# One width of column tile for all products of a long convolution's main loop

## The chip, the cores and the metric

The kernel runs on one core of one Trainium2 chip. The metric is the device time of one execution in microseconds (us); lower is better.

## What is computed

Two parts follow each other. The first is a long convolution along the sequence, with a filter that a small network makes from positional features; the second lets a small expert network act on the 128 highest-scoring tokens of each batch.

```python
B, S, D = 4, 12608, 128                      # batch, sequence, channels; filter features 64
h_filt = (np.maximum(pos_emb @ w1, 0) @ w2) * np.exp(-0.01 * pos)[:, None]
u = x * v
y = irfft(rfft(u, n=2 * S, axis=1) * rfft(h_filt, n=2 * S, axis=0), n=2 * S, axis=1)[:, :S]
out = x * y                                  # [4, 12608, 128]

for b in range(B):                           # expert part, on x = out
    scores = x[b] @ w_gate
    top = np.argpartition(-scores, 128)[:128]
    xe = x[b, top]
    out[b, top] = xe + sigmoid(scores[top])[:, None] * (np.maximum(xe @ moe_w1, 0) @ moe_w2)
```

All of it is in float32.

## The kernel before, in words

The transforms are done as products with tables of sines and cosines. The length is factored as 101 x 250, so a transform has a stage over 101 points and one over 250 points, and real tables (sums of cosine and sine) keep it real. The 128 channels are taken in 32 groups of four, and with four batches that makes 128 iterations of the main loop, numbered t.

At the start the filter is made (`h_hid`, lines 254 to 334) and transformed (`h_spec`, lines 336 to 400); its spectra go to DRAM.

The main loop (lines 963 to 1024) is a pipeline written out by hand. In the iteration t TensorE gets, in this order:

- `f_i(t - 3)` (line 453), the inverse product of the group of three iterations before. For each of four channels and two halves (8 pairs) the helper `mm2` (line 237) multiplies a slice `sd[:, e, s]` of 101 columns, as the weights, with the table `ci_sb[:, e]` of 126 columns, as the moving operand. It does so in two parts: 51 columns to the PSUM partitions from 0 (line 240), and 50 columns to the partitions from 64 (line 241).
- `dft(t)` (line 243), the second stage: for each of two tables w, two halves of the 404 moving columns and two parities e, one product with 64 weight columns, to the partitions from 0 or from 64 (line 248).
- a small product of the background work, if one is due (`tots`, line 587, by way of `mm2`): while `spare` is set (lines 970 to 978), its result goes to the last 64 columns of two PSUM banks.
- `f_s1(t + 1)` (line 402), the first stage of the next group: for four channels and four blocks of 32 (the last has 29) weight columns one product of 202 moving columns, to the partitions from 0, 32, 64 and 96 (line 408).

In what follows these are called I (inverse), D (second stage) and S (first stage). A float32 product appears in the profile as two loads of weights and two matmul instructions. A product whose weights take at most 64 or 32 columns occupies only a column tile of that width of the TensorE array, and products in different column tiles run side by side.

The other engines work beside this. ScalarE copies from PSUM: D's second table (line 251), S's results in two halves (line 410), I's result into the large buffer `ay` (line 466). VectorE combines and multiplies with the filter's spectrum (lines 414, 417, 422, 423, 428, 429). GpSimd multiplies x and v (line 231) and prepares the inverse's input (lines 435 and 436). SyncE issues loads, some iterations ahead.

After each batch (32 inverse products) a phase between batches follows (class `P1`, lines 471 to 568): it takes the last transform stage from `ay` with the table `gx_sb` (lines 510 and 515, 64-wide column tiles), multiplies with x, writes the output and computes the scores. The rows of `ay` and of `gx_sb` stand in the partition layout that the inverse product leaves, which `_split` (line 66) gives to the table.

The search for the 128 highest scores of a batch (`TopKS`, `select`, `place`, lines 596 to 828) is spread as background work over the following batch's iterations by `Background` (line 572): each of its steps is a short piece on ScalarE, VectorE or GpSimd, and most rounds need one small product on TensorE between D and S. The last batch's search and the experts run at the end.

Of the kernel before, what the change touches and what calls it, by code (L numbers as in the profile page):

```python
# [18 lines left out]
NQ = 64  # L19
N1, N2, N3 = 101, 250, 125  # L20
N = N1 * N2
NJ = N2 // 2 + 1
# [14 lines left out]
LAG = 3  # L37
NU, NV, NX, NH = 4, 2, 4, 3
PR = 52
JH, KH = (N3 + 1) // 2, (N1 + 1) // 2  # L40
PJ = (N3 + 1) // 2
NC, CO = 4, 2
NE = 3
# [17 lines left out]
def _cas(m, n):  # L61
    t = 2.0 * np.pi * (m % n) / n
    return np.cos(t) + np.sin(t)


def _split(a, h):
    s = np.zeros((128,) + a.shape[1:])
    s[:h] = a[:h]
    s[NQ:NQ + len(a) - h] = a[h:]
    return s  # L70


def _grid():
    return (N3 * np.arange(N1)[:, None] + N1 * np.arange(N3)[None, :]) % (N1 * N3)


def _steps():
    j = np.arange(N3)
    first = -(-(N1 * N3 - N1 * j) // N3)
    blk = [slice(32 * k, min(32 * k + 32, N3)) for k in range(NB)]  # L80
    return first, [(c, int(first[c].min()), int(first[c].max())) for c in blk]


def _tables():
    kap = np.arange(N1) - N1 // 2
    idx = _grid()
    r1, r3 = idx[:, 0] % N1, idx[0] % N3
    rho, chi = (-1.0) ** np.arange(N1), (-1.0) ** (np.arange(N3) + r3)
    c1 = np.zeros((128, 1 + NB, N1))
    c1[:N1, 0] = _cas(r1[:, None] * kap[None, :], N1)  # L90
    alt = rho[:, None] * c1[:N1, 0]
    for k, (c, lo, hi) in enumerate(_steps()[1]):
        c1[:hi, 1 + k], c1[hi:N1, 1 + k] = alt[:hi], -alt[hi:]
        c1[N1:N1 + hi - lo, 1 + k] = -2 * alt[lo:hi]
    g = _cas(kap[:, None] * N2 * np.arange(GW)[None, :], N1)
    gx = _split(np.concatenate([g, -g], axis=1), KH)
    r = np.arange(NK)
    cf = np.zeros((N3, 2, 2, NQ))
    for e in range(2):
        ang = 2.0 * np.pi * ((r3[:, None] * (2 * r + e)[None, :]) % N2) / N2  # L100
        cf[:, 0, e, :NK] = np.cos(ang)
        cf[:, 1, e, :NK] = np.sin(ang)
    j = np.arange(NJ)
    ci = np.zeros((128, 2, NJ))
    for e in range(2):
        k = 2 * r + e
        wk = np.where((k == 0) | (k == N3), 0.5, 1.0)[:, None] / (2 * N)
        ang = 2.0 * np.pi * ((k[:, None] * j[None, :]) % N2) / N2
        ci[e * NQ:e * NQ + NK, 0] = np.cos(ang) * wk
        ci[e * NQ:e * NQ + NK, 1] = np.sin(ang) * wk  # L110
    fold = np.zeros((128, 2, NQ))
    fold[:JH] = cf[:JH, 0]
    fold[NQ:NQ + JH] = cf[:JH, 1]
    cf[:, :, 1] *= chi[:, None, None]
    win = np.exp(np.float32(-0.01) * np.arange(N1 * N3, dtype=np.float32))
    sg = np.where(idx % N2 < N3, 1.0, -1.0).astype(np.float32)
    wm = np.zeros((N1, 3, N3), np.float32)
    wm[:, 0] = np.where(idx < S, win[idx], 0.0)
    wm[:, 1] = sg
    wm[:, 2] = wm[:, 0] * sg  # L120
    p = np.arange(128)
    tk = np.zeros((128, 2 * 128 + 2 + 36 + NJ + 40), np.float32)
    tk[:, :128] = p[:, None] < p[None, :]
    tk[:, 128:256] = p[None, :]
    tk[:, 256] = NJ * np.where(p < NQ, p, np.maximum(p - NQ + PR, 0))
    tk[:, 257] = p + 1
    steps = np.array([[i << sh for i in range(4)] for sh in range(14, -1, -2)])
    steps = np.concatenate([steps, steps[:1] - 32768])
    tk[:, 258:294] = steps.reshape(1, -1)
    tk[:, 294 + NJ:] = np.concatenate([-steps[:8], 0.5 - steps[8:], 0.5 - steps[:1]]).reshape(1, -1)  # L130
    tk[:, 294:294 + NJ] = np.where(_valid(), -NEG, NEG)
    f = np.float32
    cf = np.concatenate([cf.reshape(N3, 4, NQ), np.zeros((128 - N3, 4, NQ))])
    return (fold.astype(f), c1.astype(f), gx.astype(f), cf.astype(f), ci.astype(f), wm, tk, np.zeros((NQ - PR, NX * 8 * D), f))
# [11 lines left out]
def _valid():  # L146
    ok = _index() < S
    ok[NQ:, 0] = ok[NQ:, NJ - 1] = False
    return ok
# [3 lines left out]
def hyena_moe(ctx, tc, xg, x2, pos, bw, ww, wg, mw1, mw2, fo, c1, gx, cf, ci, wm, tk, zr, out):  # L153
    nc = tc.nc
# [17 lines left out]
    def buf(name, k, shape):  # L172
        o, n, w = OFF[name]
        return view(arena, o + k % n * w, shape)
# [7 lines left out]
    def ps1(k, shape, name):  # L182
        return view((*bank1, *bank2[::2])[k], 0, shape)

    def ps2(k, shape, name):
        return view(bank2[k], 0, shape)
# [5 lines left out]
    cf_sb = cp.tile([128, 4, NQ], F32, name="cf_sb")  # L192
    ci_sb = cp.tile([128, 2, NJ], F32, name="ci_sb")
# [40 lines left out]
        if t < B * NG:  # L234
            nc.sync.dma_start(buf("ht", t, [128, 2 * HC]), hd[:, t % NG])

    def mm2(o, lhsT, rhs, h=NQ, **kw):
        kw = kw or dict(start=True, stop=True)
        m = lhsT.shape[1]
        nc.tensor.matmul(o[:h], lhsT=lhsT[:, :h], rhs=rhs, **kw)  # L240
        nc.tensor.matmul(o[NQ:NQ + m - h], lhsT=lhsT[:, h:], rhs=rhs, **kw)  # L241

    def dft(t, te, pq):
        for w in (1, 0):
            for h in range(2):
                c = slice(h * 2 * N1, (h + 1) * 2 * N1)
                for e in range(2):
                    nc.tensor.matmul(pq[w][e * NQ:(e + 1) * NQ, c], lhsT=cf_sb[:, 2 * w + e], rhs=te[:, e, c],  # L248
                                     start=True, stop=True)
        qs = buf("qs", t, [128, HC])  # L250
        nc.scalar.copy(out=qs, in_=pq[1])  # L251
        return qs
# [166 lines left out]
    def f_m(t, uv):  # L419
        ht = buf("ht", t, [128, 2, HC])  # L420
        mt = buf("mt", t, [128, 2, HC])
        nc.vector.tensor_tensor(out=mt, in0=uv, in1=ht[:, 0].unsqueeze(1).to_broadcast([128, 2, HC]), op=ALU.mult)  # L422
        nc.vector.tensor_tensor(out=uv, in0=uv, in1=ht[:, 1].unsqueeze(1).to_broadcast([128, 2, HC]), op=ALU.mult)  # L423
        return mt
# [28 lines left out]
    def f_i(t, sd):  # L453
        if t == B * NG - 1:
            for h in range(2):
                o3 = ps1(h, [128, 2, 256], f"o3_{t}_{h}")
                for s in range(2):
                    for e in range(2):
                        mm2(o3[:, s, e * NJ:(e + 1) * NJ], sd[:, e, 2 * h + s], ci_sb[:, e], KH)
                nc.scalar.copy(out=ay[:, t % NG, :, 2 * h:2 * h + 2], in_=o3[:, :, :2 * NJ].rearrange("p s x -> p x s"))  # L460
            return
        o3 = ps2(1 if t == B * NG - 2 else 2, [128, 4, 256], f"o3_{t}")
        for s in range(4):
            for e in range(2):
                mm2(o3[:, s, e * NJ:(e + 1) * NJ], sd[:, e, s], ci_sb[:, e], KH)
        nc.scalar.copy(out=ay[:, t % NG], in_=o3[:, :, :2 * NJ].rearrange("p s x -> p x s"))  # L466

    hbs = [(ja, min(HB, NJ - ja)) for ja in range(0, NJ, HB)]
# [101 lines left out]
    spare = [None]  # L570
# [16 lines left out]
    def tots(rhs, lhs, n, nm, k):  # L587
        parts = []
        for i, a in enumerate(range(0, n, NS) if spare[0] else (0,)):
            z = min(a + NS, n) if spare[0] else n  # L590
            ps = spare[0][i] if spare[0] else ps1(k, [128, 512], nm)
            mm2(ps[:, :z - a], lhs, rhs[:, a:z])
            parts.append((slice(a, z), ps[:, :z - a]))
        return parts
# [364 lines left out]
    te, uv, ys, sd, ph = {}, {}, {}, {}, {}  # L959
# [3 lines left out]
    for t in range(NT + LAG):  # L963
        g = t % NG
        i = t - LAG
        if 0 <= i:
            f_i(i, sd.pop(i))
        if t < NT:
            pq = ps2(1 - t % 2, [128, 2, 512], f"pq_{t}")
            spare[0] = [a[:, 512 - NS:] for a in bank1]  # L970
            uv[t] = pq[:, :, :HC]
            bg.now = t
            qs = dft(t, te.pop(t), (uv[t][:, 0], uv[t][:, 1]))
            bg.hook("p", 1)
            bg.hook("n", 1)
# [8 lines left out]
            o = t - 1 in uv  # L984
            if o:
                m = f_m(t - 1, uv[t - 1])
# [92 lines left out]
```

## Time and profile before

| | |
|---|---|
| median of 3 runs | 958.93 us (958.32 to 960.0) |
| the profiled execution's own time | 956.99 us |
| its span, first to last instruction | 955.2 us |
| TensorE clock granted, mean over the span | 0.989 |
| TensorE busy | 922.2 us, 15782 matmul instructions |
| VectorE, ScalarE, GpSimd busy | 824.8, 625.2, 633.1 us |
| moved by DMA | 194.44 MB |

In lines of the profile, PE is TensorE's matmuls and PEld its loads of weights, which overlap the matmuls; DVE is VectorE, ACT ScalarE, POOL GpSimd, SP SyncE. L408 is line 408 of the kernel. A group's line shows the result and the operands by the program's names, partitions x elements and type, the number of instructions after the x, then busy time in us, the mean length of one in ns, and the engine's idle time ahead of them with what ended it. In the timeline, a row holds a start, a length and how many instructions were merged; the bracket at its end is idle time before it and what ended it. The end of a matmul's record is modelled, and matmuls are pipelined, so starts are more to be trusted than ends.

### The profile page before, as it was taken

How to read it: one execution, taken by the hardware profiler on the slowest of the kernel's cores; microseconds unless marked ns; L12 is line 12 of the kernel's file. 1: busy time of each engine (PE TensorE's matmuls, PEld its weight loads, DVE VectorE, ACT ScalarE, POOL GpSimd, SP SyncE). 2: the span in 40 equal slices, each digit the busy share in tenths (PEclk: the TensorE clock that was granted, in tenths of full speed). 3: DMA queues.
4: the chain of work that ended last, by engine and by line, in shares of the span. 5: the costliest groups of instructions: out<-in, count | busy, mean ns of one | idle time of the engine just before them, and what ended most of it. 6: DMA issues, size and time to landing. Idle time of an engine off the chain costs nothing.

```text
span 955.2 us, 38707 instructions
## 1 busy us (share of the span) xinstructions
PE 922.2 (97%) x15782; PEld 763.7 (80%) x15782; DVE 824.8 (86%) x1585; ACT 625.2 (65%) x2085; POOL 633.1 (66%) x597
## 2 busy tenths in 40 slices
PE   7999999999999999999999999999999999999965
PEld 4788767777789987877799777777998878779954
DVE  5999988888889888889898888898998888987983
ACT  4755545555548987865578878755698878556930
POOL 2898556666669666667698466677893666767710
PEclk8999999999999999999999999999999999999997
DMA  7044587656777866567767666668687666765820
GB/s 217 21 175 177 207 279 187 231 197 195 234 221 237 277 213 213 196 197 230 236 223 271 221 197 199 198 202 266 199 272 248 197 199 191 226 180 156 270 80 7
DMA packets 81911, 194.44 MB, mean 204 GB/s; under 512 B 10697, under 2 KB 47662, under 8 KB 81710
## 3 DMA queue, kind: packets, MB, share of 16 engines
q1 hardware_dynamic: 81478, 191.45, 61.7%
q8 instruction: 124, 2.03, 0.9%
q0 software_dynamic: 256, 0.52, 0.2%
q14 instruction: 53, 0.43, 0.1%
HBM read 151.59 MB, written 40.34 MB: 201 GB/s over the span
## 4 chain that ended last, share of the span: by engine, by line
PE 87%; DMA 5%; DVE 4%; ACT 2%; issue 1%; SPq 0%; POOL 0%; POOLq 0%; DVEq 0%; ACTq 0%
PE c L240 24%; PE a L408 20%; PE c L248 18%; PE a L515 6%; PE c L384 3%; PE c L515 3%; PE a L364 3%; PE c L364 3%; PE a L510 2%; DMA arena<-in_x_dram 2%; DMA out_dram<-arena 2%; PE c L241 1%; DVE ms L636 1%; PE c L510 1%; DMA arena<-in_pos_dram 1%
## 5 line engine op out<-in xcount | busy, mean ns | idle before, releaser
L435 POOL TENSOR_TENSOR arena<-arena 128x404 f32<-128x404 f32 x127 | 123.1, 969 | 228.1 <-DVE arena L429 193.4
L240 PEld LDWEIGHTS c<-ci_sb,arena 128*51 128x51 f32 x2032 | 213.8, 125 | 44.8 <-issue 20.0
L240 PE MATMUL c<-ci_sb,arena 128*51 128x126 f32 x2032 | 245.3, 273 | 4.3 <-ACT big L466 2.3
L241 PE MATMUL c<-ci_sb,arena 128*50 128x126 f32 x2032 | 245.2, 273 | 0.0
L241 PEld LDWEIGHTS c<-ci_sb,arena 128*50 128x50 f32 x2032 | 213.6, 124 | 0.0
L408 PE MATMUL a<-c_sb,arena 128*32 128x202 f32 (+1 forms) x4096 | 202.7, 336 | 0.0
L248 PE MATMUL c<-arena,cf_sb 128*64 128x202 f32 x2048 | 198.2, 334 | 1.1 <-ACT arena L410 1.1
L466 ACT COPY big<-c 128x1008 f32<-128x1008 f32 x127 | 125.7, 990 | 96.7 <-PE c L241 93.5
L410 ACT COPY arena<-a 128x404 f32<-128x404 f32 x256 | 127.5, 498 | 74.6 <-PE a L408 74.5
L408 PEld LDWEIGHTS a<-c_sb,arena 128*32 128x32 f32 (+1 forms) x4096 | 120.4, 108 | 60.4 <-issue 17.8
L231 POOL TENSOR_TENSOR arena<-arena 128x500 f32<-128x500 f32 x128 | 161.1, 1259 | 9.2 <-DMA arena<-in_xg_dram 9.2
L248 PEld LDWEIGHTS c<-arena,cf_sb 128*64 128x64 f32 x2048 | 141.2, 136 | 25.2 <-ACT arena L410 2.8
L547 ACT ACTIVATE arena<-arena 128x128 f32<-128x128 f32 x496 | 147.2, 298 | 18.3 <-DVE arena L545 15.5
L498 POOL TENSOR_TENSOR arena<-big 128x512 f32<-128x512 f32 x112 | 139.9, 1275 | 10.2 <-ACT big L460 2.8
L422 DVE TENSOR_TENSOR arena<-c,arena 128x808 f32<-128x808 f32 x127 | 126.8, 998 | 3.9
L417 DVE TENSOR_TENSOR c<-c,arena 128x404 f32<-128x404 f32 x128 | 75.0, 586 | 61.4 <-ACT arena L251 61.4
L423 DVE TENSOR_TENSOR c<-c,arena 128x808 f32<-128x808 f32 x127 | 126.7, 998 | 0.0
L436 POOL TENSOR_TENSOR arena<-arena 128x404 f32<-128x404 f32 x127 | 123.5, 972 | 0.0
L515 PE MATMUL a<-big,gx_sb 128*64 128x128 f32 x1536 | 97.0, 273 | 0.7 <-ACT big L460 0.7
L547 ACT ACTIVATION_READ_ACCUMULATOR arena<-arena 128x1 f32 x496 | 92.7, 187 | 0.0
L251 ACT COPY arena<-c 128x404 f32<-128x404 f32 x128 | 63.5, 496 | 39.0 <-PE c L248 34.4
L515 PEld LDWEIGHTS a<-big,gx_sb 128*64 128x64 f32 x1536 | 86.2, 137 | 2.1 <-ACT arena L410 1.0
(198 smaller groups left out, 1407.0 us busy)
## 6 DMA issues: line engine op xcount, KB each, us to landing
arena<-in_xg_dram SPq DMA_DIRECT2D x256, 250.0 KB
arena<-hd SPq DMA_DIRECT2D x128, 404.0 KB
arena<-in_x_dram SPq DMA_DIRECT2D x120, 208.0 KB
out_dram<-arena SPq DMA_DIRECT2D x120, 208.0 KB
hd<-arena SPq DMA_DIRECT2D x32, 404.0 KB
arena<-in_pos_dram SPq DMA_DIRECT2D x15, 202.0 KB
arena<-in_x_dram SPq DMA_DIRECT2D x8, 156.0 KB
out_dram<-arena SPq DMA_DIRECT2D x8, 156.0 KB
```

Source lines behind the costliest of these rows:

```text
L231: nc.gpsimd.tensor_tensor(out=x, in0=x, in1=v, op=ALU.mult)
L240: nc.tensor.matmul(o[:h], lhsT=lhsT[:, :h], rhs=rhs, **kw)
L241: nc.tensor.matmul(o[NQ:NQ + m - h], lhsT=lhsT[:, h:], rhs=rhs, **kw)
L248: nc.tensor.matmul(pq[w][e * NQ:(e + 1) * NQ, c], lhsT=cf_sb[:, 2 * w + e], rhs=te[:, e, c], start=True, stop=True)
L408: nc.tensor.matmul(tps[s // 2][c, s % 2], lhsT=u[:, s, c], rhs=c1_sb[:, 0:k + 2:k + 1], start=True, stop=True)
L410: nc.scalar.copy(out=te[:, :, 2 * h:2 * h + 2].rearrange("p e s i -> p s e i"), in_=tps[h])
L422: nc.vector.tensor_tensor(out=mt, in0=uv, in1=ht[:, 0].unsqueeze(1).to_broadcast([128, 2, HC]), op=ALU.mult)
L423: nc.vector.tensor_tensor(out=uv, in0=uv, in1=ht[:, 1].unsqueeze(1).to_broadcast([128, 2, HC]), op=ALU.mult)
L466: nc.scalar.copy(out=ay[:, t % NG], in_=o3[:, :, :2 * NJ].rearrange("p s x -> p x s"))
L498: nc.gpsimd.tensor_tensor(out=cm[e][:, :n].rearrange("p j (g s) -> p j g s", s=4), in0=av[0], in1=av[1], op=op)
L515: nc.tensor.matmul(ps[t * NQ:(t + 1) * NQ, k], lhsT=gx_sb[:, o:o + NQ], rhs=ay[:, :, e * NJ + j], start=e == 0, stop=e == 1)
L547: nc.scalar.activation(out=wx[:, k], in_=wx[:, k], func=AF.Copy, accum_out=self.sc[:, ja + k:ja + k + 1])
```

## The change

All products of I, D and S use column tiles that are 32 wide.

- I: a slice of 101 weight columns is multiplied in four parts of 26, 25, 25 and 25 columns, to the partitions from 0, 32, 64 and 96, by the new helper `mm4`. `_split` gives the table `gx` the same layout of rows.
- D: for each table there are four products of 32 weight columns, each with all 404 moving columns of its parity, in place of two halves with two products of 64 weight columns each.
- The small products of the background work take four parts of 32 columns while `spare` is set (in the main loop), and two parts of 64 elsewhere, as before.

```diff
+KQ = [slice(int(c[0]), int(c[-1]) + 1) for c in np.array_split(np.arange(N1), 4)]
-def _split(a, h):
+def _split(a):
     s = np.zeros((128,) + a.shape[1:])
-    s[:h] = a[:h]
-    s[NQ:NQ + len(a) - h] = a[h:]
+    for k, c in enumerate(KQ):
+        s[32 * k:32 * k + c.stop - c.start] = a[c]
     return s
...
-    def mm2(o, lhsT, rhs, h=NQ, **kw):
+    def mm2(o, lhsT, rhs, **kw):
         kw = kw or dict(start=True, stop=True)
-        m = lhsT.shape[1]
-        nc.tensor.matmul(o[:h], lhsT=lhsT[:, :h], rhs=rhs, **kw)
-        nc.tensor.matmul(o[NQ:NQ + m - h], lhsT=lhsT[:, h:], rhs=rhs, **kw)
+        w = 32 if spare[0] else NQ
+        for a in range(0, 128, w):
+            nc.tensor.matmul(o[a:a + w], lhsT=lhsT[:, a:a + w], rhs=rhs, **kw)
+
+    def mm4(o, lhsT, rhs):
+        for k, c in enumerate(KQ):
+            nc.tensor.matmul(o[32 * k:32 * k + c.stop - c.start], lhsT=lhsT[:, c], rhs=rhs, start=True, stop=True)
 
     def dft(t, te, pq):
         for w in (1, 0):
-            for h in range(2):
-                c = slice(h * 2 * N1, (h + 1) * 2 * N1)
-                for e in range(2):
-                    nc.tensor.matmul(pq[w][e * NQ:(e + 1) * NQ, c], lhsT=cf_sb[:, 2 * w + e], rhs=te[:, e, c],
-                                     start=True, stop=True)
+            for a in range(0, 128, 32):
+                nc.tensor.matmul(pq[w][a:a + 32], lhsT=cf_sb[:, 2 * w + a // NQ, a % NQ:a % NQ + 32],
+                                 rhs=te[:, a // NQ], start=True, stop=True)
...
         for s in range(4):
             for e in range(2):
-                mm2(o3[:, s, e * NJ:(e + 1) * NJ], sd[:, e, s], ci_sb[:, e], KH)
+                mm4(o3[:, s, e * NJ:(e + 1) * NJ], sd[:, e, s], ci_sb[:, e])
```

The last group's inverse, which is done in two halves, changes in the same way.

More of the change, by code (lines that the diff above doesn't have):

```diff
@@ L39 @@
 PR = 52
-JH, KH = (N3 + 1) // 2, (N1 + 1) // 2
+JH = (N3 + 1) // 2
 PJ = (N3 + 1) // 2
@@ L95, in _tables @@
     g = _cas(kap[:, None] * N2 * np.arange(GW)[None, :], N1)
-    gx = _split(np.concatenate([g, -g], axis=1), KH)
+    gx = _split(np.concatenate([g, -g], axis=1))
     r = np.arange(NK)
@@ L458, in f_i @@
                     for e in range(2):
-                        mm2(o3[:, s, e * NJ:(e + 1) * NJ], sd[:, e, 2 * h + s], ci_sb[:, e], KH)
+                        mm4(o3[:, s, e * NJ:(e + 1) * NJ], sd[:, e, 2 * h + s], ci_sb[:, e])
                 nc.scalar.copy(out=ay[:, t % NG, :, 2 * h:2 * h + 2], in_=o3[:, :, :2 * NJ].rearrange("p s x -> p x s"))
```

## The prediction

> **What bounds the kernel now.** I read the page first, then one iteration of the main loop in the timeline, then groups of instructions by shape, the list of waits, and busy time by window.
>
> ```profile
> span 955.2 us, 38707 instructions
> PE 922.2 (97%) x15782; PEld 763.7 (80%) x15782; DVE 824.8 (86%) x1585; ACT 625.2 (65%) x2085; POOL 633.1 (66%) x597
> PE 87%; DMA 5%; DVE 4%; ACT 2%; issue 1%; SPq 0%; POOL 0%; POOLq 0%; DVEq 0%; ACTq 0%
> ```
>
> TensorE is busy 97% of the span and holds 87% of the chain that ended last. A busy TensorE isn't one that streams all the time, so I look inside an iteration (timeline, TensorE alone; columns are start and length in us):
>
> ```profile
> 200.77 1.58 PE L408 MATMUL a<-c_sb,arena 128*32 128x202 f32 x32
> 202.28 0.31 PE L240 MATMUL c<-ci_sb,arena 128*51 128x126 f32 x1
> ...
> 202.43 0.27 PE L240 MATMUL c<-ci_sb,arena 128*51 128x126 f32 x1
> ...
> 203.94 0.27 PE L240 MATMUL c<-ci_sb,arena 128*51 128x126 f32 x1
> ...
> 204.05 1.54 PE L248 MATMUL c<-arena,cf_sb 128*64 128x202 f32 x16
> 205.51 1.58 PE L408 MATMUL a<-c_sb,arena 128*32 128x202 f32 x32
> ```
>
> Start to start, the first stage S (L408, four column tiles of 32) takes 202.28 - 200.77 = 1.51 us, the inverse I (L240 and L241, two tiles of 64) 1.77, the second stage D (L248, two tiles of 64) 1.46: 4.74 us in all. Each float32 product is two matmul instructions, so S is 8 rounds of four tiles (32 instructions), D is 8 rounds of two (16), and I is 16 rounds of two.
>
> What would the streaming alone take? The mean lengths by shape tell:
>
> ```profile
> L240 PE MATMUL c<-ci_sb,arena 128*51 128x126 f32 x2032 | 245.3, 273 | 4.3 <-ACT big L466 2.3 <-POOL arena L435 1.6 <-POOL arena L436 0.5
> L408 PE MATMUL a<-c_sb,arena 128*32 128x202 f32 x3072 | 202.7, 337 | 0.0
> L241 PE MATMUL a<-st,onesb 128*64 128x3 bf16 x48 | 8.0, 166 | 0.0
> ```
>
> 76 more columns cost 337 - 273 = 64 ns, so a column costs 0.842 ns: a round of 202 columns streams in 0.170 us, one of 126 in 0.106. The rest of a record is latency that overlaps the next round. Inside I the rounds stand (203.94 - 202.43) / 14 = 0.108 us apart, so there the estimate holds. D and S should take 8 x 0.170 = 1.36 each and I 16 x 0.108 = 1.73, together 4.45. The measured 4.74 has 0.29 more: 0.10 at the end of D, 0.15 in S, 0.04 in I's first round (202.28 to 202.43 is 0.15, not 0.108).
>
> Two rows show that this loss belongs to the joint between tile widths. In the phase between batches, two 64-wide lines alternate:
>
> ```profile
> 300.56 1.04 PE L515 MATMUL a<-big,gx_sb 128*64 128x128 f32 x16
> 301.43 0.61 PE L510 MATMUL a<-arena,gx_sb 128*64 128x128 f32 x8
> 301.87 1.04 PE L515 MATMUL a<-big,gx_sb 128*64 128x128 f32 x16
> 302.74 0.61 PE L510 MATMUL a<-arena,gx_sb 128*64 128x128 f32 x8
> ```
>
> 8 rounds of 128 columns in 0.87 us and 4 in 0.44: 0.109 a round by 0.842 x 128 = 0.108, nothing lost at the joints. And in iterations with a background step, a tiny 64-wide product stands between D and S:
>
> ```profile
> 404.13 1.54 PE L248 MATMUL c<-arena,cf_sb 128*64 128x202 f32 x16
> 405.50 0.17 PE L240 MATMUL a<-st,onesb 128*64 128x3 bf16 x1
> ...
> 405.60 1.58 PE L408 MATMUL a<-c_sb,arena 128*32 128x202 f32 x32
> ...
> 408.88 0.34 PE L248 MATMUL c<-arena,cf_sb 128*64 128x202 f32 x2
> ```
>
> D lasts 405.50 - 404.13 = 1.37 when a 64-wide product follows it, against 1.46 when a 32-wide one does. So 0.1 us is lost where 64 goes over to 32, and as much where 32 goes over to 64. The waits of the weight loads count these joints:
>
> ```profile
> PEld c L240 <- issue: 20.2, 63, 0.3
> PEld a L408 <- issue: 17.8, 63, 0.3
> PEld c L240 <- POOL arena L231: 15.9, 49, 0.3
> PEld a L408 <- POOL arena L436: 10.0, 54, 0.3
> ```
>
> 117 times a load of S and 112 times a load of I came up to 0.3 us late, whatever releaser the view names.
>
> **The change, part by part.** *Joints.* With I, D and S all 32 wide, both joints of an iteration go. Worth: 117 x 0.10 (D to S) + 112 x (0.15 + 0.04) (S to I) = 11.7 + 21.3 = 33 us. The Trainium skill (TensorEngine Tiling, section Tiling Modes, Key Properties) says that a change of tiling mode drains TensorE; this trace agrees with its 0.10 and 0.19 us, and the sum uses these.
>
> *D.* Eight rounds of two tiles and 202 columns become four rounds of four tiles and 404 columns: 4 x 404 x 0.842 = 1.36 us, as now; 16 loads and 16 matmuls as now. Zero. The copy that waits for D (L251) starts after D's last matmul: the last round starts 0.17 us earlier than now and its record is 0.17 longer, so L251 stays where it is, counted from D's start.
>
> *I.* Sixteen rounds of two tiles become sixteen of four (26, 25, 25, 25 columns). Streamed columns are unchanged, but 32 + 32 instructions become 64 + 64. What must hold is 8 instructions per 0.108 us, 13.5 ns each, and no row of before shows that over a whole stage. From below the round is 0.106 (streaming). From above: S, with four tiles, issues 64 instructions in 1.36 us, 21 ns each, and at that rate a round takes 0.170. I take 0.108, because S shows that four tiles don't lengthen a round: 1.36 / 8 = 0.170 with four, 1.37 / 8 = 0.171 with two. And where instructions stand ready, they go out much faster. This is the window of 60 ns from 205.50:
>
> ```profile
> 205.51 0.15 PEld L408 LDWEIGHTS a<-c_sb,arena 128*32 128x32 f32 x7 [0.30 <-issue]
> 205.51 0.38 PE L408 MATMUL a<-c_sb,arena 128*32 128x202 f32 x4
> ```
>
> Eleven instructions in some 50 ns. So the 21 ns of S is its streaming and not a rate of issue. For the range I use up to 0.118 a round, a tenth more: 16 x 0.010 x 118 = 19 us.
>
> *The small products of the background step* (48 iterations by the row of 48 above, and a few longer ones) become 32 wide in four parts. Today they hide in the drain: that iteration is 408.88 - 404.13 = 4.75, as long as a plain one. With the drain gone they stand in the open: between 0 and the 0.10 from 405.50 to 405.60, in which the switch is still included. I take 0.04: 48 x 0.04 = 2 us. At 64 wide they would bring two switches, about 0.2.
>
> *The phase between batches* stays 64 wide, so where it hands over to I there is now a joint that wasn't: nearest row S to I, 0.15 + 0.04, three times, 0.6 us. The constants' rows in gx and the rows of the copied inverse move with the parts; no instruction is added for that.
>
> *What is late next.* An iteration shrinks to about 4.46 (4.50 with a background step). Busy time by window, for a plain iteration, one with a background step, and the ten that hold a selection:
>
> ```profile
> 204.05:208.80 4.75, 4.75 (x85) 3.70 (x83) 3.96 (x7) 2.49 (x4) 3.11 (x4) 1.00 0.61 201
> 404.13:408.88 4.75, 4.75 (x86) 3.80 (x84) 4.13 (x9) 4.02 (x14) 3.11 (x4) 1.00 0.58 188
> 418.39:466.32 47.93, 47.93 (x822) 38.05 (x820) 43.53 (x82) 25.02 (x41) 34.48 (x36) 1.00 0.72 226
> ```
>
> The columns are length, then PE, PEld, DVE, ACT, POOL, the clock, the share and rate of DMA. DVE needs 3.96 and 4.13 (ACT 4.02), so 0.3 stays free. The ten iterations become 47.9 - 2.7 = 45.2 against 43.5 of DVE, still free on the whole, but single ones are full. DVE may run late there without holding TensorE much: 1 us in all. DMA moves 201 GB/s in 61% of the time and would move 6% more. In a background iteration ACT's order is the tight place:
>
> ```profile
> 404.63 0.98 ACT L466 COPY big<-c 128x1008 f32<-128x1008 f32 x1
> 405.72 0.50 ACT L251 COPY arena<-c 128x404 f32<-128x404 f32 x1
> 406.25 0.59 DVE L417 TENSOR_TENSOR c<-c,arena 128x404 f32<-128x404 f32 x1 [0.32 <-ACT arena L251]
> 407.09 0.17 DVE L708 SCALAR_TENSOR_TENSOR st<-a,tk_sb 128x3 f32<-128x3 f32 x1 [0.26 <-ACT arena L410]
> ```
>
> L466 ends at 405.61 and L251 starts at 405.72. Up to 0.1 us of lateness of L251 would come out of DVE's idle 0.32 and 0.26, not out of TensorE's time.
>
> *Sum.* 33 - 2 - 0.6 - 1 = 29.4, taken as 30 because the ten longer background products (a few rounds each) lose a drain as well. The profiled execution took 956.99 us (span 955.2 and 1.8 around it), so it would take 927; the median of the runs is 958.9, 0.2% above it, so the forecast is **929 us**.
>
> **Rivals.** *A, slower: TensorE's issue becomes I's bound.* It decides from where an instruction takes more than (1.73 + 0.29) / 128 = 15.8 ns over the stage. For it: the fastest whole stages of before issue 64 instructions in about 1.4 to 1.5 us,
>
> ```profile
> 54.56 1.61 PE L364 MATMUL a<-c_sb,arena 101*63 101x101 f32 x32
> 56.09 0.92 PE L384 MATMUL c<-arena 63*64 63x202 f32 x16
> ```
>
> here 32 matmuls and as many loads in 1.53 us. Against it: this stage streams 16 x 101 x 0.842 = 1.36 anyway, and the burst above. Price at S's 21 ns: I takes 2.69, an iteration 0.67 more than now, 118 x 0.67 = 79: 1038 us. Chance 9%. The Trainium skill (TensorEngine Tiling, Instruction Overhead) puts about 60 cycles on each matmul, 25 ns by its clock of 2.4 GHz; for matmuls alone I would need 64 x 25 = 1.6 us and still fit, with the loads charged too 3.2 us, and the kernel would be near 1100. The seven loads and four matmuls in 60 ns speak against that reading.
>
> *B, no change: the joints stay.* If the late load at a joint came from a semaphore, as the POOL names in the waits suggest, nothing would go, and the background product would even cost: 957 to 960 us. Against it: I to D also waits for another engine's semaphore, and loses nothing (203.94 to 204.05 is a normal 0.11). Chance 6%.
>
> *C, a slower round.* Four parts lengthen I's round to 0.118 to 0.130, with half or all of the gain eaten: 948 to 970. Chance 11%, most of it below 957.
>
> **How the numbers follow.** Forecast 74%, A 9%, B 6%, C 11%. From below, 33 us, no cost for background products and rounds of 0.106 (118 x 0.03 = 3.5) give 37, 921.9 us, taken as 921. From above the forecast reaches C's 948. Range 921 to 948, which leaves out A, B and C's tail. About 0.2% is what a measurement here can tell from no change. Faster by more: 74 + 8 of C + 2 of B = 84%. Within: 5%. Slower: A and 2 of C, 11%.
>
> **What would show it.** Right: in the timeline of after, D, S and I of about 1.36, 1.37 and 1.73 us, an iteration of 4.46; no idle of 0.3 before the first loads of S and I; D as long before S as before a background product. Wrong: rounds of I over 0.118 (A or C), the 0.1 still there at the joints (B), or TensorE idle in front of D with DVE or ACT named as releaser.

## The result and the profile after

The changed kernel takes 929.03 us (median of 4 runs, 926.76 to 932.16); beside it the kernel before took 959.46 (4 runs, 958.32 to 962.25). The ratio is 0.968, interval 0.964 to 0.972. The profiled execution took 927.64 us, against 956.99 before: 29.35 less. Measured a second time, beside other variants, the changed kernel took 931.38 us (6 runs) against 958.82, ratio 0.972 (0.970 to 0.974).

The page of the changed kernel: the span, the busy times, the queue that carries instructions (packets, MB, share of 16 DMA engines), and the shares of the chain that ended last.

```profile
span 925.9 us, 47199 instructions
...
PE 892.9 (96%) x20028; PEld 813.4 (88%) x20028; DVE 824.1 (89%) x1585; ACT 624.1 (67%) x2085; POOL 634.6 (69%) x597
...
q8 instruction: 157, 2.57, 1.1%
...
PE 87%; DMA 5%; DVE 4%; issue 2%; ACT 2%; SPq 0%; POOL 0%; POOLq 0%; DVEq 0%; ACTq 0%
```

TensorE has 4246 more matmuls and is busy for 29 us less; the other engines do what they did. The chain is as much TensorE's as before. One row is worth remembering for later: 2 x 20028 instructions (matmuls and loads) in 157 packets are 255 to a packet, and 2.57 MB / 157 are 16.4 KB each. With the 314 further instructions of TensorE that the trace has (semaphores, drains) it is 257. So TensorE's instructions arrive in chunks of some 256.

One iteration in the timeline, TensorE alone (start, length, operation, number of instructions):

```profile
132.96 1.57 PE L253 MATMUL c<-arena,cf_sb 128*32 128x404 f32 x16
134.31 1.61 PE L413 MATMUL a<-c_sb,arena 128*32 128x202 f32 x32
135.68 1.97 PE L248 MATMUL c<-ci_sb,arena 128*26 128x126 f32 x64
137.41 1.59 PE L253 MATMUL c<-arena,cf_sb 128*32 128x404 f32 x16
```

Start to start, D takes 134.31 - 132.96 = 1.35, S 1.37, I 1.73: the streaming times, with nothing left at the joints. Sixteen rounds of I with four tiles last as long as sixteen with two did.

Busy time by window (length, then PE, PEld, DVE, ACT, POOL, the clock, DMA's share and rate) for a plain iteration, one with a background step, and the ten that hold a selection:

```profile
202.40:206.87 4.47, 4.47 (x120) 4.39 (x115) 3.96 (x7) 2.49 (x4) 3.12 (x4) 1.00 0.87 289
389.47:393.97 4.50, 4.50 (x124) 4.28 (x119) 4.14 (x9) 3.99 (x13) 3.12 (x4) 1.00 0.64 209
411.94:457.00 45.06, 45.06 (x1153) 43.59 (x1148) 42.89 (x78) 24.95 (x41) 34.14 (x36) 1.00 0.80 244
```

TensorE is busy all the time in each; VectorE has 45.06 - 42.89 = 2.2 us left over the ten iterations, and no stage of them waits for it.

The list of waits of the weight loads, whole run (total, times, longest):

```profile
PEld c L253 <- issue: 8.3, 44, 0.2
PEld a L413 <- issue: 5.7, 29, 0.3
...
PEld c L248 <- issue: 2.8, 9, 0.5
```

Before, loads of S came late 117 times and loads of I 112 times, by up to 0.3 us. Now it is 29 and 9. The 44 short waits ahead of D are new, but a load that comes 0.2 us later stops nothing here: the matmuls of the stretches above are busy without a gap. The 0.5 in the last row is new too; it falls into the iterations that zr_split, below, is about.

### The profile page after: what moved, and what is told of

Read it like the earlier page. It is cut to its first block, busy times and chain, and to the rows that moved or that the text cites. A ratio compares the mean times of both kernels' runs of the same rounds, so it can differ in the third digit from the quotient of the medians.

```text
span 925.9 us, 47199 instructions
## 1 busy us (share of the span) xinstructions
PE 892.9 (96%) x20028; PEld 813.4 (88%) x20028; DVE 824.1 (89%) x1585; ACT 624.1 (67%) x2085; POOL 634.6 (69%) x597
## 3 DMA queue, kind: packets, MB, share of 16 engines
q8 instruction: 157, 2.57, 1.1%
## 4 chain that ended last, share of the span: by engine, by line
PE 87%; DMA 5%; DVE 4%; issue 2%; ACT 2%; SPq 0%; POOL 0%; POOLq 0%; DVEq 0%; ACTq 0%
PE c L248 23%; PE a L413 20%; PE c L253 18%; PE a L520 7%; PE c L520 3%; PE c L389 3%; PE a L369 3%; PE c L369 3%; PE a L515 3%; DMA out_dram<-arena 2%; DVE ms L641 1%; PE c L515 1%; DMA arena<-in_wm_dram 1%; DMA arena<-in_x_dram 1%; PE c L244 1%
## 5 line engine op out<-in xcount | busy, mean ns | idle before, releaser
L248 PE MATMUL c<-ci_sb,arena 128*26 128x126 f32 x8128 | 269.2, 271 | 4.8 <-ACT big L471 2.1
L248 PEld LDWEIGHTS c<-ci_sb,arena 128*26 128x26 f32 x8128 | 250.2, 104 | 10.0 <-ACT big L471 3.3
L413 PE MATMUL a<-c_sb,arena 128*32 128x202 f32 (+1 forms) x4096 | 223.9, 334 | 0.0
L253 PE MATMUL c<-arena,cf_sb 128*32 128x404 f32 x2048 | 220.4, 502 | 2.2 <-ACT arena L415 1.3
L413 PEld LDWEIGHTS a<-c_sb,arena 128*32 128x32 f32 (+1 forms) x4096 | 186.5, 108 | 18.5 <-issue 5.7
L253 PEld LDWEIGHTS c<-arena,cf_sb 128*32 128x32 f32 x2048 | 119.0, 109 | 22.2 <-issue 8.3
L422 DVE TENSOR_TENSOR c<-c,arena 128x404 f32<-128x404 f32 x128 | 75.0, 586 | 37.8 <-ACT arena L256 37.5
L550 DVE TENSOR_TENSOR arena<-arena,c 128x512 f32<-128x512 f32 x124 | 83.9, 678 | 0.2 <-ACT arena L552 0.2
L419 DVE TENSOR_TENSOR c<-c,arena 128x404 f32<-128x404 f32 x128 | 74.3, 580 | 0.1
```

The source lines that it names most:

```text
L248: nc.tensor.matmul(o[32 * k:32 * k + c.stop - c.start], lhsT=lhsT[:, c], rhs=rhs, start=True, stop=True)
L253: nc.tensor.matmul(pq[w][a:a + 32], lhsT=cf_sb[:, 2 * w + a // NQ, a % NQ:a % NQ + 32], rhs=te[:, a // NQ], start=True, stop=True)
L413: nc.tensor.matmul(tps[s // 2][c, s % 2], lhsT=u[:, s, c], rhs=c1_sb[:, 0:k + 2:k + 1], start=True, stop=True)
```

## The experiments

The theory after the result: the 0.29 us of an iteration were lost at the joints between column tiles of 32 and of 64, and the change gains because no joint is left. Rivals: the four parts of I, or the long moving operand of D, are faster by themselves. A second question is how near rival A of the prediction is: what does TensorE's issue bear?

### One stage at a time: i_only and d_only

In i_only, D and the small products go back to tiles of 64; I and S are 32 wide.

```diff
-        w = 32 if spare[0] else NQ
+        w = NQ
...
-            for a in range(0, 128, 32):
-                nc.tensor.matmul(pq[w][a:a + 32], lhsT=cf_sb[:, 2 * w + a // NQ, a % NQ:a % NQ + 32],
-                                 rhs=te[:, a // NQ], start=True, stop=True)
+            for h in range(2):
+                c = slice(h * 2 * N1, (h + 1) * 2 * N1)
+                for e in range(2):
+                    nc.tensor.matmul(pq[w][e * NQ:(e + 1) * NQ, c], lhsT=cf_sb[:, 2 * w + e], rhs=te[:, e, c],
+                                     start=True, stop=True)
```

> Only the inverse I is cut into four 32-wide parts; D and the small background products stay 64 wide as before the change. Joint theory: the joint S to I goes (0.19 us), but I to D becomes a new one of the same kind (32 to 64, 0.15 to 0.19 us), and D to S stays, so an iteration stays at 4.70 to 4.76 us and the time at 955 to 961 us. Rival 'narrow tiles are faster by themselves': I is one of the two stages made narrow, so about half of the gain, 940 to 947 us. Rival 'the long moving operand of D': no gain without D, 957 to 961 us, so this run doesn't tell it from the joints. If four parts lengthened I's round, the time would lie over 961 us.

It took 961.16 us (10 runs), ratio 1.002 (1.0005 to 1.0035), far from the rival's 940 to 947 and 0.2 us above the range, where a longer round of I had been the sign; but I's round is 0.108 us in the changed kernel too. An iteration of it in the timeline:

```profile
205.01 1.59 PE L255 MATMUL c<-arena,cf_sb 128*64 128x202 f32 x16
206.53 1.58 PE L415 MATMUL a<-c_sb,arena 128*32 128x202 f32 x32
207.92 1.92 PE L248 MATMUL c<-ci_sb,arena 128*26 128x126 f32 x64
209.77 1.59 PE L255 MATMUL c<-arena,cf_sb 128*64 128x202 f32 x16
```

D 1.52, S 1.39, I 1.85: 4.76, the old total. S has lost its extra time to I, whose next neighbour, D, now is the one of another width. The joint has moved.

In d_only, I goes back to two parts of 51 and 50 columns, while D and the small products stay 32 wide.

```diff
-KQ = [slice(int(c[0]), int(c[-1]) + 1) for c in np.array_split(np.arange(N1), 4)]
+KQ = [slice(int(c[0]), int(c[-1]) + 1) for c in np.array_split(np.arange(N1), 2)]
...
-            nc.tensor.matmul(o[32 * k:32 * k + c.stop - c.start], lhsT=lhsT[:, c], rhs=rhs, start=True, stop=True)
+            nc.tensor.matmul(o[NQ * k:NQ * k + c.stop - c.start], lhsT=lhsT[:, c], rhs=rhs, start=True, stop=True)
```

> Only D (four products of 404 columns) and the small background products are 32 wide; I stays in two 64-wide parts. Joint theory: D to S has no joint any more, I to D gets one (64 to 32, 0.10 us and a longer first round), S to I keeps its own: an iteration of about 4.75 us, 956 to 963 us. Rival 'the long moving operand of D' or 'narrow D': the whole gain, 928 to 932 us, or the half of it, 940 to 947 us.

959.31 us (10 runs), ratio 1.0004 (0.9985 to 1.0022). The timeline:

```profile
203.64 1.56 PE L253 MATMUL c<-arena,cf_sb 128*32 128x404 f32 x16
205.02 1.56 PE L413 MATMUL a<-c_sb,arena 128*32 128x202 f32 x32
206.51 1.94 PE L248 MATMUL c<-ci_sb,arena 128*51 128x126 f32 x32
208.37 1.56 PE L253 MATMUL c<-arena,cf_sb 128*32 128x404 f32 x16
```

D, with its 404 columns and beside S of the same width, takes 1.38; S 1.49 and I 1.86 hold the two joints now. Neither part alone gains anything, so neither the four parts of I nor the long moving operand of D is faster by itself; only both together take the last joint away.

### A 64-wide speck in a 32-wide loop: tots64

Only the small products of the background step go back to 64.

```diff
-        w = 32 if spare[0] else NQ
+        w = NQ
```

> The changed kernel, but the small background products stay 64 wide, in two parts. Joint theory: the 48 iterations with a round of the search and 9 with a longer product get two joints each, 0.15 to 0.25 us in an iteration: 48 such iterations of 4.65 to 4.70 instead of 4.50 us, the time 937 to 943 us. If width did not matter at a joint: 928 to 930 us.

941.32 us (4 runs), ratio 0.9816 (0.9795 to 0.9836). A background iteration in the timeline:

```profile
394.74 1.55 PE L253 MATMUL c<-arena,cf_sb 128*32 128x404 f32 x16
396.22 0.20 PE L244 MATMUL a<-st,onesb 128*64 128x3 bf16 x2
396.34 1.58 PE L413 MATMUL a<-c_sb,arena 128*32 128x202 f32 x32
397.73 1.92 PE L248 MATMUL c<-ci_sb,arena 128*26 128x126 f32 x64
399.46 1.55 PE L253 MATMUL c<-arena,cf_sb 128*32 128x404 f32 x16
```

Two tiny products bring the iteration from 4.50 to 4.72, where 4.65 to 4.70 was expected. D lasts 1.48 instead of 1.35, and S starts 0.12 after them. 48 such steps at 0.22 are 10.6 us of the 12.3 between the two medians. It is the change of width that costs, not the work: the same product in four parts of 32 costs an iteration 0.03.

### More instructions: d_halves

D keeps its tiles of 32 but does its 404 columns in two halves: as many columns, twice the instructions in D, 256 in an iteration instead of 224.

```diff
-            for a in range(0, 128, 32):
-                nc.tensor.matmul(pq[w][a:a + 32], lhsT=cf_sb[:, 2 * w + a // NQ, a % NQ:a % NQ + 32],
-                                 rhs=te[:, a // NQ], start=True, stop=True)
+            for h in range(2):
+                c = slice(h * 2 * N1, (h + 1) * 2 * N1)
+                for a in range(0, 128, 32):
+                    nc.tensor.matmul(pq[w][a:a + 32, c], lhsT=cf_sb[:, 2 * w + a // NQ, a % NQ:a % NQ + 32],
+                                     rhs=te[:, a // NQ, c], start=True, stop=True)
```

> The changed kernel, but D multiplies two halves of 202 moving columns with four 32-wide weights each (twice the instructions, eight rounds of four tiles instead of four). Joint theory: streamed columns and widths are the same, so an iteration of 4.46 to 4.49 us and 928 to 932 us. Rival 'the long moving operand of D': most of the gain is lost, 945 to 959 us.

A miss: 962.3 us (10 runs), ratio 1.0034 (1.0015 to 1.0054). All the gain is gone, although the undisturbed iteration is 4.48, as expected. By the time alone this looks like the rival, the long moving operand; but by that rival every iteration would be longer, and d_only had the long operand without a gain. What is lost lies in stops: 41 of the iterations hold some, 33 us together. One in the timeline:

```profile
164.99 0.84 PE L415 MATMUL a<-c_sb,arena 128*32 128x202 f32 x10
168.33 1.06 PE L415 MATMUL a<-c_sb,arena 128*32 128x202 f32 x19 [2.50 <-issue]
```

In the middle of S, 2.50 us pass with nothing to wait for that the profile shows. The DMA view of 135 to 275 us has the two queues that matter, data and instructions:

```profile
q1 hardware_dynamic: 13130, 29.01, 70.5%
q8 instruction: 29, 0.48, 1.4%
```

At 4.48 us an iteration and 256 instructions in each, these 140 us need 140 / 4.48 = 31.3 chunks; 29 came. That alone proves nothing, for a TensorE that stands still needs fewer instructions, but it suggests a second theory: the chunks share the DMA engines with the data, and one that comes late stops TensorE (supply). Its rival: the doubled instructions of D stop TensorE in some way of their own, whatever DMA carries.

### Less data beside the instructions: after_noh and d_halves_noh

Take away the load of the filters' spectra (404 KB in every iteration) from the moment all of their buffers have been filled.

```diff
     def load_h(t):
-        if t < B * NG:
+        if t < NH:
```

> The changed kernel without 404 KB of the 904 KB that each iteration loads: after the first three groups the filter spectrum isn't loaded again, and later groups are multiplied with the spectra that lie in the three buffers, so the result isn't the convolution. It is the control for the next run. The transfers aren't on the path that sets the end: 925 to 929 us. If late instruction chunks (theory of supply) cost the changed kernel some 2 us, they go: 925 to 927.

> The changed kernel with D in halves of 202 columns (256 TensorE instructions in an iteration in place of 224), and again without the reloads of the filter spectrum after the first three groups (later groups use the spectra that lie there). Theory of supply: TensorE's instructions arrive in chunks of 16 KB (256 instructions) over the same DMA engines as the data, a chunk that waits behind data comes late, and TensorE stands still; with 45% less data the stops mostly go: 929 to 938 us. Theory of issue: TensorE itself can't take 256 instructions in 4.48 us: 955 to 964 us, as with the loads. Theory of a fetch with a limit of its own, whatever the data: 955 to 964 us too.

after_noh: 927.45 us (4 runs), ratio 0.9678 (0.9653 to 0.9702). d_halves_noh: 932.86 (4 runs), ratio 0.976 (0.972 to 0.980). The control, after_noh, has the changed kernel's ratio, 0.968: fewer loads gain nothing that the runs can tell. But d_halves_noh, with the same instructions as d_halves, got some 29 us back, and the stops shrank to about 5 us in 8 iterations. Busy time by window over the same 140 us, first d_halves, then d_halves_noh:

```profile
135.00:275.00 140.00, 134.27 (x3766) 129.68 (x3762) 115.90 (x178) 72.99 (x118) 90.49 (x87) 0.99 0.72 211
```

```profile
135.00:275.00 140.00, 138.92 (x3955) 136.82 (x3946) 122.27 (x186) 76.98 (x125) 96.92 (x93) 1.00 0.46 132
```

DMA's rate falls from 211 to 132 GB/s, and TensorE's idle time from 140 - 134.27 = 5.7 us to 1.1. Nothing on TensorE was changed between the two, so its stops come by way of the transfers. The theory of issue falls, and so does that of a fetch that can't bear 256 instructions in 4.48 us whatever the data.

### Twice the instructions in I: i_halves and i_halves_noh

I's 126 moving columns in two halves of 63: 256 instructions in I, 352 in an iteration, streamed columns unchanged. It puts rival A to the test at twice the rate of issue.

```diff
-        for k, c in enumerate(KQ):
-            nc.tensor.matmul(o[32 * k:32 * k + c.stop - c.start], lhsT=lhsT[:, c], rhs=rhs, start=True, stop=True)
+        n = NJ // 2
+        for j in range(0, NJ, n):
+            for k, c in enumerate(KQ):
+                nc.tensor.matmul(o[32 * k:32 * k + c.stop - c.start, j:j + n], lhsT=lhsT[:, c], rhs=rhs[:, j:j + n], start=True, stop=True)
```

> The changed kernel with I's moving operand in two halves of 63 columns: 256 instructions in I (8 in 0.053 us, 6.6 ns each), 352 in an iteration. Theory of supply: where TensorE had stopped, chunks of 256 followed each other every 4.2 to 4.3 us, so an iteration takes about 352 / 256 x 4.27 = 5.9 us and the time is 1050 to 1130 us, with stops inside all stages. Rival A of the prediction (issue at S's 21 ns): I alone takes 5.4 us, an iteration 8.1 us, 1300 to 1400 us, with I slow throughout. If neither binds: 930 to 940 us.

> As the run before, without the reloads of the filter spectrum after the first three groups (later groups use the spectra that lie there). Theory of supply: less data in front of the chunks, clearly below the run before, 940 to 1080 us, and between stops I's rounds at 0.053 to 0.06 us. Theory of issue: the same time as the run before.

i_halves: 1147.65 us (2 runs), ratio 1.198 (1.194 to 1.203). i_halves_noh: 1089.62 (2 runs), ratio 1.138 (1.134 to 1.142). Both lie a little above what supply expected (1050 to 1130 and 940 to 1080), so the sizes were missed, and far below rival A's 1300 to 1400. The timeline of i_halves_noh shows both things at once:

```profile
196.35 2.16 PE L250 MATMUL c<-ci_sb,arena 128*26 128x63 f32 x128
198.30 0.85 PE L255 MATMUL c<-arena,cf_sb 128*32 128x404 f32 x6
201.02 0.55 PE L255 MATMUL c<-arena,cf_sb 128*32 128x404 f32 x4 [1.87 <-issue]
```

128 matmuls and as many loads start within 198.30 - 196.35 = 1.95 us, 7.6 ns each. Rival A needed 15.8 ns to do harm and 13.5 to be felt. Then D stands still for 1.87 us after its sixth matmul, with nothing to wait for that the profile shows.

The chunks in 135 to 275 us of each kernel, by the DMA view. "Asked for" is 140 / 4.48 iterations, times the instructions of one, by 256:

| kernel | instructions an iteration | chunks asked for | chunks that came | data, GB/s (all DMA) |
|---|---|---|---|---|
| changed kernel | 224 | 27.3 | 27 | 225 |
| d_halves | 256 | 31.3 | 29 | 211 |
| d_halves_noh | 256 | 31.3 | 31 | 132 |
| i_halves | 352 | 43 | 30 | 155 |
| i_halves_noh | 352 | 43 | 34 | 100 |

Two of the rows it is made from, first of the changed kernel, then of i_halves_noh:

```profile
q8 instruction: 27, 0.44, 1.3%
```

```profile
q8 instruction: 34, 0.56, 1.6%
```

With all the data loads in place none of these kernels got more than 30 chunks in 140 us, one in 140 / 30 = 4.7 us; with the spectra's loads gone it was 34, one in 4.1 us. The changed kernel asks for 27, nine tenths of what was to be had.

The counts can't tell cause from effect, but the place of the stops in the instruction stream can. Count all of TensorE's instructions in a trace from its first one, in blocks of 256 (the first one recorded need not be the first of a chunk). Of the stops of over 0.5 us in the main loop, 25 of 29 in d_halves (28.4 of 32.4 us), 98 of 125 in i_halves and 90 of 100 in i_halves_noh come right after the 193rd instruction of a block; the others are spread. After these stops TensorE goes on 2.4 us (median, in all three) after the start of the last packet of q8. So where TensorE stands still, it is mostly at one and the same place of a chunk, and a packet brings it on: these stops are waits for the next chunk.

That even beside little data there is only one chunk in 4.1 us was not expected. In i_halves_noh the next packet starts 1.6 us (median) after TensorE has gone on, and TensorE goes on 2.4 us after a packet's start: 4.0 together. So a fetch does show a limit of its own, at about 4.1 us a chunk. d_halves_noh, which needs one in 4.48, stays under it; i_halves_noh, which asks for one in 140 / 43 = 3.3, does not. Why the next packet doesn't start sooner was not tried.

The Trainium skill (Runtime: NRT & Kernel Launch, Instruction fetch mechanics) says that a sequencer fetches its instructions in blocks of 16 KiB, 256 instructions, by a DMA queue of its own; the 255 instructions and 16.4 KB of a packet agree. It calls the cost of a block's boundary "mostly hidden". Here it is all but hidden at 27 blocks in 140 us with all the loads in place, and at 31 only without the spectra's.

### The stops in the changed kernel: zr_split

If supply is right, two long iterations of the changed kernel itself, 4.82 and 4.92 us between 165 and 175 us, are late chunks. The DMA view of 158.5 to 165.5 us, just ahead of them, has no row of q8 in 7 us, in a kernel that asks for a chunk every 5.1:

```profile
q1 hardware_dynamic: 353, 1.10, 92.1%
...
arena<-in_zr_dram SPq DMA_DIRECT2D x2, 192.0 KB
```

This queue's transfers keep the DMA engines busy for 92% of the time but move only 1.10 MB. What is special there is the last row: two loads of zr, issued once. In zr_split they become eight of 48 KB over four steps.

```diff
-            if t == 8:
+            if t in range(6, 6 + 2 * NX, 2):
+                k = (t - 6) // 2 * 8 * D
                 for r in (PR, NQ + PR):
-                    nc.sync.dma_start(arena[r:r + NQ - PR, OFF["xa"][0]:OFF["xa"][0] + NX * 8 * D], zr)
+                    nc.sync.dma_start(arena[r:r + NQ - PR, OFF["xa"][0] + k:OFF["xa"][0] + k + 8 * D], zr[:, k:k + 8 * D])
```

> The changed kernel, and the two loads of zeros of 192 KB each that the ninth iteration issues become eight of 48 KB in four iterations. Theory of supply: the two holes of 0.4 and 0.5 us in TensorE's row at 167 and 173 us, which were there in both profiles of the changed kernel, are gone, iterations 10 and 11 take 4.47 us each, 0.8 us in all; the median 0 to 2 us below the changed kernel's 929 to 931. If the holes had nothing to do with these loads, they stay.

The view of the same 7 us:

```profile
q1 hardware_dynamic: 726, 1.61, 75.0%
q8 instruction: 1, 0.02, 1.1%
```

The chunk comes, and the two iterations take 4.47 each. The kernel took 927.73 us (5 runs), ratio 0.968 (0.965 to 0.971). It has the lower median, but its interval overlaps with that of the changed kernel (0.964 to 0.972), so a gain of a microsecond stays open. The changed kernel, measured a second time,

> The changed kernel itself, beside the two that follow: 926 to 931 us.

showed the same two holes, at 167 and 172 us: they belong to the kernel and not to one execution. Both holes of the first profile, too, come after the 193rd instruction of a block.

### Another joint: pairs and pairs_zr

The preparation of the filters' spectra has a joint in each group as well: a first product (L369) with column tiles of 64 over all rows, and a second (L389) with tiles of 64 x 64. The changed kernel's timeline there:

```profile
81.44 1.61 PE L369 MATMUL c<-c_sb,arena 101*63 101x101 f32 x32
82.98 0.92 PE L389 MATMUL c<-arena 63*64 63x202 f32 x16
83.82 0.39 PE L369 MATMUL a<-c_sb,arena 101*63 101x101 f32 x4
```

A group takes 1.54 + 0.84 = 2.38 us where streaming alone is 16 x 0.085 + 4 x 0.17 = 2.04. Two first products together, then two second ones, would halve the joints. pairs does that; pairs_zr has zr_split's edit as well.

```diff
         fwd(0)
+        fwd(1)
         for g in range(NG):
-            if g + 1 < NG:
+            if g and g % 2 == 0:
+                fwd(g)
                 fwd(g + 1)
```

> The changed kernel, and in the transform of the filter two groups' first products (column tiles of 64 over all rows) are issued one after the other, and then two groups' second products (64 x 64 tiles), so that the kind of tile changes half as often. Joint theory: a group of 2.38 us holds 0.18 and 0.16 us of joints, half of which goes, 0.17 us; VectorE's 45.2 us busy in 48.4 allow 0.15: 30 groups, 3 to 4.5 us, 923 to 926 us where the changed kernel has 928 to 929. If the joints were a matter of the main loop's waits alone: the same as the changed kernel.

> As pairs, and the two loads of zeros of 192 KB each, which the ninth iteration issues, become eight of 48 KB in four iterations. Theory of supply: the late chunk at 165 us, two holes in TensorE's row of 0.4 and 0.5 us, goes: 0.5 to 1 us below pairs in a profile, hardly to be told in the medians. Otherwise the same as pairs.

A miss: pairs took 935.91 us (6 runs), ratio 0.975 (0.973 to 0.978), slower than the changed kernel's 931.38 beside it; pairs_zr 933.43 (5 runs), ratio 0.974 (0.972 to 0.977), an interval that overlaps with that of pairs. pairs_zr doesn't have the two long iterations that pairs has from 169.8 us on (4.72 and 5.20), as supply would have it. The timeline of pairs:

```profile
86.70 1.61 PE L369 MATMUL a<-c_sb,arena 101*63 101x101 f32 x32
88.14 1.56 PE L369 MATMUL c<-c_sb,arena 101*63 101x101 f32 x32
89.62 0.92 PE L391 MATMUL c<-arena 63*64 63x202 f32 x16
90.95 0.92 PE L391 MATMUL c<-arena 63*64 63x202 f32 x16 [0.41 <-DVE arena L399]
91.80 0.39 PE L369 MATMUL a<-c_sb,arena 101*63 101x101 f32 x4
```

The first product before one of its own kind takes 1.44 instead of 1.54, so a joint did go. But the second L391 waits for VectorE, and the pair takes 91.80 - 86.70 = 5.10 against 2 x 2.38 = 4.76; the next one takes 4.88, and so on in turn. From the first L369 to the last L391 the whole stage takes 80.5 us, where the changed kernel's takes 76.9: 3.6 of the 4.5 between the medians. The rest stays open. Read so, a first product between two second ones was the cover under which VectorE and ScalarE did their part.

## Why the prediction held

**The joints** (33 us in the sum). Right in mechanism and size. A plain iteration fell from 4.750 to 4.468 us (medians, counted from the last matmul of S to the next; predicted 4.46), and i_only, d_only and tots64 show that it is the joints: each leaves or makes a pair of them, and each has 0.22 to 0.29 us to show for it. The Trainium skill's rule that a change of tiling mode drains TensorE (TensorEngine Tiling, Tiling Modes) agrees with these prices; that what is lost is a drain no row shows.

**I's round** (rival A and C). 1.73 us for 128 instructions, 0.108 a round, as taken. i_halves_noh did 256 in 1.95, so there was room to twice the rate. The argument by the burst of eleven instructions in 50 ns was sound. What it left out is where the instructions come from. Supply, a neighbour of A, costs next to nothing at this kernel's 224 instructions an iteration and the whole gain at 256, and the prediction did not have it as a rival. That the change stayed on the good side of it was, as far as the prediction goes, luck.

**D at no cost.** Right: 1.35. The moving operand's length changes next to nothing in streaming (d_halves, 4.48 undisturbed). It does matter by the count of instructions: two halves gave all of the gain back.

**The small products.** Iterations with a background step take 4.500 (predicted 4.50), 0.03 more than a plain one where 0.04 was taken. That they had to be made 32 wide as well, at a price put at about 0.2 each, was shown by tots64: 0.22.

**VectorE late in the select iterations** (1 us). Wrong: 45.06 us for ten against 45.2, no wait. In its place stood a term that the sum did not have, stops by late chunks, about 1.7 us in six iterations. Two of the longest are those that zr_split takes away.

**The sum.** By the measured terms, 70 plain iterations x 0.282 + 48 x 0.255 = 32.0, less 1.7 of stops is 30.3, where the profiled difference is 29.35. The traces don't close the account more finely. From the first matmul of S to that of the last iteration they show 733.2 us before and 701.6 after, 31.6 less, while what lies ahead and behind took 0.7 and 1.5 us longer in the profile of after. The second profile of the changed kernel has 703.1 for the loop, and 1.5 less behind it. So one profile differs from another by 1.5 us in either part. The 0.6 for the joints of the phase between batches can't be seen in that: the three intervals with a phase in them sum to 143.0 before and 143.4 after.

The mechanism and its size were right, and they are the 33 of the sum. That 929 met 929.03 is closer than the terms and the runs allow, and partly luck: the microsecond for VectorE did not come, one and a half for late chunks had not been counted, and the second measurement gave 931.38.

## What to carry to other kernels

Where stages follow each other on TensorE without a pause, compare starts with what the columns take to stream: an excess that sits at the border of two stages with different tile widths goes when all of them, the smallest included, take one width. Each change of width that is left keeps its price: two stages out of three gained nothing here, and the small product alone kept 12 of the 30 us. Before you split a product further, count TensorE's instructions per microsecond against the instruction queue's packets: at 224 in 4.47 us beside its 904 KB of loads this kernel had a tenth to spare, and a seventh more, 256, cost all of the 30 us. An interleaving that costs a joint may be the cover of another engine's work, so price the wait behind it first.

## What the hardware showed that was not expected

- TensorE's instructions come by DMA beside the data, some 256 in a packet of 16.4 KB. Where TensorE was short of them, one came in 4.7 or 4.8 us on average over 140 us (155 to 211 GB/s in all), or in 4.1 (100 GB/s). Two loads of 192 KB held one up in the changed kernel.
- The granted clock was low around stops. In d_halves, the stretch with the 2.50 us stop has 0.88 granted, by window (the clock is the first number after POOL's). No run tried whether the stop brings it:

```profile
161.00:175.00 14.00, 11.50 (x276) 10.65 (x270) 8.01 (x13) 5.37 (x9) 6.98 (x7) 0.88 0.80 232
```

- Four column tiles of one width run on their own. In the changed kernel's timeline around a background step, one tile is still in D while another has done the small product and is in S:

```profile
388.90 0.17 PE L244 MATMUL a<-st,onesb 128*32 128x3 bf16 x1
388.91 0.50 PE L253 MATMUL c<-arena,cf_sb 128*32 128x404 f32 x1
388.93 0.34 PE L413 MATMUL a<-c_sb,arena 128*32 128x202 f32 x1
```

That may be why a joint between equal widths costs nothing: there is no moment at which all tiles have to be done. No run tried it by itself.
